# Another layout of keys for seven of sixteen head pairs, a fourth tile for the attention weights, and weight loads issued by ScalarE

## The chip, the cores and the metric

The kernel runs on one core of a Trainium2 chip. The metric is the time of one execution in microseconds (us), as the device measures it; of several executions the median counts. A profile of one execution, taken by the hardware profiler, stands beside the times; its span runs from the first to the last recorded instruction. In it PE is TensorE's matmuls, PEld its weight loads, DVE VectorE, ACT ScalarE, POOL GpSimd, and SP SyncE, whose queue issues DMAs here. A "q" behind an engine's name (SPq) means its sequencer, which issues DMAs and waits on semaphores.

## The reference

Three stages follow each other. Cut to what matters:

```python
# q, k, v: batch 4, heads 8, sequence 576, head dimension 64
q_rot, k_rot = rotate(q), rotate(k)                      # rotary positions
scores = q_rot @ k_rot.T / 8
attn = softmax(scores)
x = (attn @ v), heads side by side                       # 2304 tokens x 512
h = x @ w_in; g = max(0.01 * h, h); x2 = g @ w_out       # 512 -> 2048 -> 512
# each token goes to the one of 8 experts with the largest logit
out[token] = gate[token] * (relu(x2 @ w1[e]) @ w2[e])    # 512 -> 1024 -> 512
```

`w_in` and `w_out` come as 64-bit floats. All matmuls are made of high and low parts, so that the result is as good as in 32-bit floats.

## The kernel before

One program in three parts. Up to about 660 us of the span it runs attention, with the first dense network ("MoE units" in the code's names, `m_...`) woven in from about 180 us on; then the rest of the dense network; from about 795 us on the experts. The change is in the first part.

Attention takes the heads in 16 pairs, `g` = 0 to 15, and each pair in nine units of 128 query rows, `u` = 0 to 8, so there are 144 units. A program written out by a planner in Python takes one step for each unit (`step`, where a string of letters sets the order inside a step). In step i it issues: the score matmuls of unit i+1 (`a_scores`), the row maximum of unit i on DVE (`a_max`), the exponentials of unit i-1 on ACT (`a_exp`), the high part of its weights on ACT (`a_hi`, into a tile `P`) and the low part on DVE (`a_lo`, into the same tile), a DMA transpose of that tile into a tile `PT` (`a_transpose`, on SP's queue), and the product with the values of unit i-4 (`a_pv`). `P` has three buffers. So the high part of one unit can't be written before the transpose of the unit three before it has read its tile.

Beside the steps, jobs run in small pieces that the planner places where its budgets for ACT, DVE and POOL (rates per step) allow:

- `prep(g)` stages a pair: it loads q, k and v (`raw`, 640 KB and 320 KB), rotates and scales q and k on POOL, DVE and ACT, and writes high and low parts, all 16-bit, into a tile `stg` of 20 blocks of 128 x 128. Two DMA transposes of ten blocks each turn it: one to `kt` (keys) and one to `stk` (queries). Each head's scores need the keys' 64 rows twice, above each other, since the stacked high and low queries fill 128 rows. So four DMAs copy from `kt` into `stk`, 160 KB each. After them `load(g + 1, 2)` issues the next pair's load.
- `weights(i)`, four of them side by side, each with one buffer `raw{i}`: they take turns at 32 slices of 512 KB, 16 of `w_in` and 16 of `w_out`. Each is loaded by a DMA on SP's queue, decoded from 64-bit floats on ACT and DVE (`decode`), scaled, and split into a high and a low part on ACT and DVE (`w_in`) or ACT and POOL (`w_out`).

Each engine works its instructions off in the order of the program. On SP's queue stand, in the planner's order, the loads of weight slices, the loads of q, k and v, the transposes of all kinds and the copies.

Of the kernel before, what the change touches and what calls it, by code (L numbers as in the profile page):

```python
# [52 lines left out]
NMERGED = 60  # L53
ADDG = 0
HI_A1 = 1
TICK2 = 3
RATE1 = dict(A=2, V=1.8, G=1.4)
RATE2 = dict(A=2, V=2.1, G=1.6)
# [43 lines left out]
def attention_moe_kernel(ctx: ExitStack, tc: tile.TileContext, qkv, w_in, w_out, emb, tau, w1, w2,  # L102
# [83 lines left out]
    def decode(raw):  # L186

        hw, lw = raw[:, :, 1], raw[:, :, 0]
        yield Piece(A=1.2, tick=M.tick + (TICK2 if M.unit else TICK))
        nc.scalar.activation(out=hw.bitcast(F32), in_=hw.bitcast(F32), func=AF.Copy, scale=2.0 ** -112)  # L190

        nc.scalar.activation(out=lw, in_=lw, func=AF.Identity, scale=2.0 ** -29 * (1 - 2.0 ** -20), bias=half)
        yield Piece(V=0.6)
        nc.vector.scalar_tensor_tensor(out=lw, in0=hw, scalar=3, in1=lw, op0=ALU.logical_shift_left, op1=ALU.bitwise_or)
        yield Piece(V=0.6)
        nc.vector.scalar_tensor_tensor(out=lw, in0=hw, scalar=0x80000000, in1=lw, op0=ALU.bitwise_and, op1=ALU.bitwise_or)
        return lw.bitcast(F32)
# [3 lines left out]
    def weights(i):  # L201
        while slices:
            f, o = slices.popleft()
            raw = wp.tile([128, 512, 2], U32, name=f"raw{i}")
            if o:
                nc.sync.dma_start(out=raw.rearrange("p f t -> p (f t)"), in_=w_out32[128 * f:128 * f + 128, :])
                r = yield from decode(raw)
                yield Piece(A=0.52)
                nc.scalar.activation(out=wo[:, 0, f], in_=r, func=AF.Copy)
                yield Piece(G=1.2)  # L210
                nc.gpsimd.tensor_tensor(out=wo[:, 1, f], in0=r, in1=wo[:, 0, f].bitcast(F32), op=ALU.subtract)
            else:
                nc.sync.dma_start(out=raw.rearrange("p (c f) t -> p c (f t)", c=4),
                                  in_=w_in32[:, 256 * f:256 * f + 256].rearrange("(c p) f -> p c f", p=128))
                w = yield from decode(raw)
                sq = small.tile([128, 1], F32, name="wsq", bufs=NW)
                yield Piece(A=0.61)
                nc.scalar.activation(out=junk[:, 0:512], in_=w, func=AF.Square, accum_out=sq)
                pb = yield from total(sq, 1)
                yield Piece(must=True, V=0.2)  # L220
                s = _pow2(nc, small, pb[:, 0:1], 1, uw[:, f:f + 1])
                nc.vector.tensor_scalar(out=uw01[:, f:f + 1], in0=uw[:, f:f + 1], scalar1=0.01, scalar2=None, op0=ALU.mult)
                hi = wi[:, 0, :, 128 * f:128 * f + 128]
                wv = w.rearrange("p (c f) -> p c f", c=4)
                if WHI:
                    yield Piece(V=0.34)
                    nc.vector.tensor_scalar(out=hi, in0=wv, scalar1=s, scalar2=None, op0=ALU.mult)
                else:
                    yield Piece(A=0.61)
                    nc.scalar.activation(out=hi, in_=wv, func=AF.Copy, scale=s)  # L230
                yield Piece(V=0.6)
                nc.vector.scalar_tensor_tensor(out=wi[:, 1, :, 128 * f:128 * f + 128], in0=wv, scalar=s, in1=hi, op0=ALU.mult, op1=ALU.subtract)
            M.wdone[o].add(f)
            yield Piece()

    def m_ready():
        if M.unit == len(munits):
# [134 lines left out]
    def prep(g):  # L372
# [34 lines left out]
            return s3  # L407


        def stacks():  # L410
            stg = qkp.tile([128, 4, 5, 128], F16, name="stg")
            s2 = stg.rearrange("p s c x -> p (s c x)")
            qhi = s2[:, 0:1408].rearrange("p (h x) -> p h x", h=2)[:, :, 0:640].rearrange("p h (c x) -> p h c x", c=5)[:, :, :, 0:64]
            return (s2, qhi, stg[:, 2].rearrange("p c (h x) -> p h c x", h=2), [stg[:, 0, :, 64:128], stg[:, 1, :, 0:64]],
                    [stg[:, 3, :, 64 * h:64 * h + 64] for h in range(2)])

        def hi(out, t):
            if g and (HIQ, HIK)[t]:
# [8 lines left out]
        if g == 0:  # L427
            rope_s(1)
            rope_s(0, nc.vector)
            for t in range(3):  # L430
                square(t)
            rope_c(0)
            add(0)
            pb = ps_h()
            nc.tensor.matmul(pb[:, 0:3], lhsT=ones, rhs=sq, start=True, stop=True)
            s3 = scales(pb)
            s2, qhi, khi, qlo, klo = stacks()
            hi(qhi, 0)
            rope_c(1)
            add(1)  # L440
            hi(khi, 1)
            lo(klo, 1, khi)
            lo(qlo, 0, qhi)
        else:
            yield Piece(A=0.72, G=1.64, at=max(i0 - EARLY, 0), tick=M.loaded + TLOAD)
            square(0)
            rope_s(0)
            yield Piece(A=0.72, V=0.74, G=1.64)
            square(1)
            rope_c(0)  # L450
            rope_s(1)
            yield Piece(A=0.72, V=0.74)
            square(2)
            add(0, nc.gpsimd if g < ADDG else nc.vector)
            yield Piece(V=0.74)
# [6 lines left out]
            s2, qhi, khi, qlo, klo = stacks()  # L462
            yield Piece(A=1.44)
            hi(qhi, 0)
            hi(khi, 1)
            yield Piece(V=0.93)
            lo(klo, 1, khi)
            yield Piece(V=0.93)
            lo(qlo, 0, qhi)
        yield Piece(at=i0 - 2)  # L470
        kt = stp.tile([128, 2, 640], F16, name="kt", bufs=1)
        nc.sync.dma_start_transpose(out=kt.rearrange("p s (c x) -> p (s c) x", c=5), in_=s2[:, 1280:2560])
        yield Piece(at=i0 - 1)

        stk = stp.tile([128, 6, 640], F16, name="stk")
        nc.sync.dma_start_transpose(out=stk[:, 0:2].rearrange("p s (c x) -> p (s c) x", c=5), in_=s2[:, 0:1280])
        for h in range(2):
            for z in range(2):
                nc.sync.dma_start(out=stk[64 * z:64 * z + 64, 2 + 2 * h:4 + 2 * h], in_=kt[64 * h:64 * h + 64])
        pairs[g] = (stk, s3, sc, v16)  # L480
        if g + 1 < 4 * B:
            load(g + 1, 2)
# [16 lines left out]
    def a_scores(g, u):  # L499
# [3 lines left out]
        for n in range(2):  # L503
            ks = slice(288 * n, 288 * n + 288)
            for h, c0, m, o in todo:
                for a in range(2):
                    nc.tensor.matmul(ps[o:o + m, n, 0:288], lhsT=stk[:, h, c0:c0 + m], rhs=stk[:, 2 + 2 * h + a, ks], start=(a == 0), stop=(a == 1))  # L507
        return ps

    def a_max(g, u, ps):  # L510
# [790 lines left out]
```

## Time and profile before

| | |
|---|---|
| median of 3 executions | 1064.49 us (1061.05 to 1064.89) |
| the profiled execution: its time, its span | 1062.26 us, 1060.5 us |
| busy over the span: PE, DVE, ACT, POOL | 83%, 73%, 71%, 34% |
| SP's DMA queue: time of its packets on 16 engines | 54.9% of the span |

The shares are means over three unlike parts. They say nothing of which engine ends a stage last; that is read from stretches of the span, given below as "A to B us", counted from its start.

### The profile page before, as it was taken

How to read it: one execution, taken by the hardware profiler on the slowest of the kernel's cores; microseconds unless marked ns; L12 is line 12 of the kernel's file. 1: busy time of each engine (PE TensorE's matmuls, PEld its weight loads, DVE VectorE, ACT ScalarE, POOL GpSimd, SP SyncE). 2: the span in 40 equal slices, each digit the busy share in tenths (PEclk: the TensorE clock that was granted, in tenths of full speed). 3: DMA queues.
4: the chain of work that ended last, by engine and by line, in shares of the span. 5: the costliest groups of instructions: out<-in, count | busy, mean ns of one | idle time of the engine just before them, and what ended most of it. 6: DMA issues, size and time to landing. Idle time of an engine off the chain costs nothing. (4 is left out here: it accounts for less than half of the span.)

```text
span 1060.5 us, 19876 instructions
## 1 busy us (share of the span) xinstructions
PE 882.0 (83%) x6737; PEld 709.4 (67%) x6737; DVE 773.9 (73%) x1564; ACT 755.8 (71%) x1439; POOL 360.6 (34%) x414
## 2 busy tenths in 40 slices
PE   1455454777888899989898899999999899999997
PEld 1344243565666787767677677778877778888885
DVE  6988798778867874767768766313476999999893
ACT  6987687777767774877777677535345888888883
POOL 1333323252443452544444533322233361211111
PEclk9995555989989999999999999999999999999999
DMA  7899889788487694696795784301152111115190
GB/s 227 192 219 243 194 165 214 171 178 196 91 163 159 120 180 98 122 177 125 140 198 126 125 162 91 66 1 41 31 180 101 40 61 40 51 50 199 34 334 33
DMA packets 269005, 141.41 MB, mean 133 GB/s; under 512 B 236248, under 2 KB 244696, under 8 KB 268897
## 3 DMA queue, kind: packets, MB, share of 16 engines
q1 hardware_dynamic: 265696, 130.11, 54.9%
q0 software_dynamic: 3200, 9.97, 2.9%
q8 instruction: 55, 0.90, 0.4%
q14 instruction: 54, 0.43, 0.1%
HBM read 120.04 MB, written 10.49 MB: 123 GB/s over the span
## 5 line engine op out<-in xcount | busy, mean ns | idle before, releaser
L266 PE MATMUL h<-xT,wi 128*128 128x256 f16 (+1 forms) x1920 | 218.2, 265 | 36.9 <-DVE g L278 31.2
L266 PEld LDWEIGHTS <-wi 128*128 128x128 f16 x1920 | 170.6, 100 | 83.5 <-issue 63.8
L286 POOL TENSOR_TENSOR gl<-g,gh 128x256 fp32r<-128x256 f32 x144 | 110.7, 769 | 317.2 <-ACT gh L282 293.5
L297 PE MATMUL acc<-wo,gh 128*128 128x512 f32 x576 | 196.6, 423 | 0.0
L531 DVE SCALAR_TENSOR_TENSOR P<-E,P 128x576 f16<-128x576 f32 x144 | 127.6, 886 | 92.7 <-ACT P L525 91.8
L552 PE MATMUL o<-v,PT 128*128 128x65 f16 (+3 forms) x1770 | 104.1, 216 | 66.3 <-DMA PT<-P 46.0
L552 PEld LDWEIGHTS <-PT 128*128 128x128 f16 (+1 forms) x1770 | 92.5, 112 | 85.2 <-DMA PT<-P 58.9
L507 PE MATMUL S<-stk 128*128 128x288 f16 (+1 forms) x640 | 115.4, 332 | 36.4 <-ACT E L519 34.5
L278 DVE SCALAR_TENSOR_TENSOR g<-h,uw,g 128x256 f32<-128x256 f32 (+1 forms) x160 | 71.2, 453 | 100.0 <-ACT g L274 99.5
L282 ACT ACTIVATE gh<-g 128x256 fp32r<-128x256 f32 x144 | 59.9, 416 | 94.7 <-DVE g L278 94.1
L525 ACT ACTIVATE P<-E 128x576 f16<-128x576 f32 x144 | 98.2, 682 | 40.1 <-DMA PT<-P 36.5
L519 ACT ACTIVATE E<-S,amx,sc 128x576 f32<-128x576 f32 x144 | 117.9, 818 | 4.9 <-DVE E L514 4.8
L274 ACT ACTIVATE g<-h,uw 128x256 f32<-128x256 f32 (+1 forms) x160 | 69.4, 444 | 72.6 <-PE h L266 68.1
L514 DVE TENSOR_SCALAR_CACHE_REDUCE E<-S,sc 128x576 f32<-128x576 f32 x144 | 116.5, 809 | 0.7 <-PE S L507 0.2
L297 PE MATMUL acc<-wo,gl 128*128 128x512 f32 x288 | 115.6, 401 | 0.0
L297 PEld LDWEIGHTS acc<-wo,gh 128*128 128x128 f32 x576 | 100.9, 193 | 18.6 <-issue 2.5
L507 PEld LDWEIGHTS <-stk 128*128 128x128 f16 (+1 forms) x640 | 58.1, 112 | 54.2 <-issue 39.2
L940 POOL DMA_INDIRECT out<-eo,idi x18 | 25.3, 1405 | 152.8 <-ACT eo L938 142.0
L390 POOL TENSOR_TENSOR t<-raw,tab 128x320 f32<-128x320 f32 x62 | 63.5, 1054 | 13.2 <-DMA raw<-in_qkv 10.1
L297 PEld LDWEIGHTS acc<-wo,gl 128*128 128x128 f32 x288 | 55.2, 192 | 13.7 <-POOL gl L286 0.9
L587 POOL TENSOR_TENSOR x<-xo,rd 128x128 f32<-128x128 f32 (+1 forms) x33 | 20.9, 632 | 102.7 <-DVE rd L579 80.3
L929 PE MATMUL h<-w,hth 128*128 128x512 f32 x176 | 55.4, 396 | 0.4 <-ACT hth L913 0.4
(232 smaller groups left out, 1754.8 us busy)
## 6 DMA issues: line engine op xcount, KB each, us to landing
rb<-in_w SPq DMA_DIRECT2D x78, 512.0 KB
ra<-in_w SPq DMA_DIRECT2D x76, 512.0 KB
stk<-kt SPq DMA_DIRECT2D x64, 160.0 KB
raw<-in_qkv SPq DMA_DIRECT2D x15, 640.0 KB
raw<-in_w_in SPq DMA_DIRECT2D x16, 512.0 KB
raw<-in_w_out SPq DMA_DIRECT2D x16, 512.0 KB
raw<-in_qkv SPq DMA_DIRECT2D x18, 320.0 KB
x2s<-x SPq DMA_DIRECT2D x18, 256.0 KB
```

Of the source, the lines that this page charges most:

```text
L266: nc.tensor.matmul(m.h[:, c0:c1], lhsT=wi[:, a, c, 128 * f:128 * f + 128], rhs=xT[j][:, 4 * b_ + c, 0:c1 - c0], start=(n == 0), stop=(n == ...
L274: nc.scalar.activation(out=m.g[:, c0:c1], in_=m.h[:, c0:c1], func=AF.Copy, scale=uw[:, f:f + 1])
L278: nc.vector.scalar_tensor_tensor(out=m.g[:, c0:c1], in0=m.h[:, c0:c1], scalar=uw01[:, f:f + 1], in1=m.g[:, c0:c1], op0=ALU.mult, op1=ALU.max)
L286: nc.gpsimd.tensor_tensor(out=m.gl, in0=m.g, in1=m.gh.bitcast(F32), op=ALU.subtract)
L297: nc.tensor.matmul(M.acc[t], lhsT=g_[:, tt], rhs=wo[:, a, f], start=(f == 0 and n == 0), stop=(f == NF - 1 and n == 2))
L390: eng.tensor_tensor(out=t2[t][:, :, :, o:o + 32], in0=raw[:, t, :, :, i:i + 32], in1=sn[:, :, o:o + 32].unsqueeze(1).to_broadcast([128, 2, ...
L507: nc.tensor.matmul(ps[o:o + m, n, 0:288], lhsT=stk[:, h, c0:c0 + m], rhs=stk[:, 2 + 2 * h + a, ks], start=(a == 0), stop=(a == 1))
L514: nc.vector.tensor_scalar(out=e.rearrange("p (a b) -> p a b", a=2), in0=ps[:, :, 0:288], scalar1=pairs[g][2][:, 1:2], scalar2=None, op0=AL ...
L519: nc.scalar.activation(out=e.rearrange("p (a b) -> p a b", a=2), in_=ps[:, :, 0:288], func=AF.Exp, scale=sc[:, 0:1], bias=mx)
L525: nc.scalar.activation(out=p[:, 0:576], in_=e, func=AF.Copy, scale=P_UP)
L531: nc.vector.scalar_tensor_tensor(out=p[:, 576:1152], in0=e, scalar=P_UP, in1=p[:, 0:576], op0=ALU.mult, op1=ALU.subtract)
L552: nc.tensor.matmul(o[ob:ob + m, oc + z:oc + z + w], lhsT=pt[:, i, q0:q0 + m], rhs=v16[:, i, h, c:c + w], start=(n == 0), stop=(n == len(to ...
```

## The change

Three edits and what they bring with them:

- Pairs 0 to 6 (`g < WIDE`) take a narrow layout. `stg` gets five groups of five blocks. The high keys of a head stand twice side by side there, the second time by a copy on DVE (`k2`); the low keys of both heads share one group. One DMA transpose of 25 blocks makes the whole of `stk`; `kt` and the four copies are gone for these pairs. The second score matmul of each couple then contracts over 64 rows (the high queries with the low keys) and no longer over 128; the number of matmuls is the same. The product of low queries and low keys, which the wide layout includes, is left out there. Pairs 7 to 15 are as before.
- The 32 loads of weight slices are issued on ACT's queue. The piece that issues one stands a tick later than before, and the piece behind it a tick less.
- `P` has four buffers.

```diff
+WIDE = 7
...
-        yield Piece(A=1.2, tick=M.tick + (TICK2 if M.unit else TICK))
+        yield Piece(A=1.2, tick=M.tick + (TICK2 if M.unit else TICK) - 1)
...
-                nc.sync.dma_start(out=raw.rearrange("p f t -> p (f t)"), in_=w_out32[128 * f:128 * f + 128, :])
+                nc.scalar.dma_start(out=raw.rearrange("p f t -> p (f t)"), in_=w_out32[128 * f:128 * f + 128, :])
...
-                nc.sync.dma_start(out=raw.rearrange("p (c f) t -> p c (f t)", c=4),
+                nc.scalar.dma_start(out=raw.rearrange("p (c f) t -> p c (f t)", c=4),
                                   in_=w_in32[:, 256 * f:256 * f + 256].rearrange("(c p) f -> p c f", p=128))
...
             M.wdone[o].add(f)
-            yield Piece()
+
+            yield Piece(tick=M.tick + 1)
...
+        wide = g >= WIDE
+
         def stacks():
-            stg = qkp.tile([128, 4, 5, 128], F16, name="stg")
+            stg = qkp.tile([128, 5, 5, 128], F16, name="stg")
...
+            khi = stg[:, 2].rearrange("p c (h x) -> p h c x", h=2) if wide else stg[:, 2:4, :, 0:64]
+            return (s2, qhi, khi, [stg[:, 0, :, 64:128], stg[:, 1, :, 0:64]],
+                    [stg[:, 3 if wide else 4, :, 64 * h:64 * h + 64] for h in range(2)], stg[:, 2:4, :, 64:128])
...
+            else:
+                yield Piece(V=1.2)
+                lo(qlo, 0, qhi)
+                nc.vector.tensor_copy(out=k2, in_=khi)
+                yield Piece(V=0.93)
+                lo(klo, 1, khi)
+        if wide:
+            yield Piece(at=i0 - 2)
+            kt = stp.tile([128, 2, 640], F16, name="kt", bufs=1)
+            nc.sync.dma_start_transpose(out=kt.rearrange("p s (c x) -> p (s c) x", c=5), in_=s2[:, 1280:2560])
         yield Piece(at=i0 - 1)
         stk = stp.tile([128, 6, 640], F16, name="stk")
-        nc.sync.dma_start_transpose(out=stk[:, 0:2].rearrange("p s (c x) -> p (s c) x", c=5), in_=s2[:, 0:1280])
-        for h in range(2):
-            for z in range(2):
-                nc.sync.dma_start(out=stk[64 * z:64 * z + 64, 2 + 2 * h:4 + 2 * h], in_=kt[64 * h:64 * h + 64])
+        if wide:
...
+        else:
+            nc.sync.dma_start_transpose(out=stk[:, 0:5].rearrange("p s (c x) -> p (s c) x", c=5), in_=s2)
...
+                else:
+                    hr = slice(64 * h, 64 * h + 64)
+                    nc.tensor.matmul(ps[o:o + m, n, 0:288], lhsT=stk[:, h, c0:c0 + m], rhs=stk[:, 2 + h, ks], start=True, stop=False)
+                    nc.tensor.matmul(ps[o:o + m, n, 0:288], lhsT=stk[hr, h, c0:c0 + m], rhs=stk[hr, 4, ks], start=False, stop=True)
...
-        p = pep.tile([128, 2 * S], F16, name="P", bufs=3)
+        p = pep.tile([128, 2 * S], F16, name="P", bufs=4)
```

The change also moves instructions. On SP's queue, where pair 3 is staged (during pair 2), there stood before:

```order
L535 DMA_TRANSPOSE PT<-P 128x9x128 x6
L472 DMA_TRANSPOSE kt<-stg 128x10x128
L213 DMA raw_1245<-in_w_in 128x4x256
L476 DMA_TRANSPOSE stk<-stg 128x10x128
L479 DMA stk<-kt 64x1280 x4
L370 DMA raw_1265<-in_qkv 128x1280
L206 DMA raw_1267<-in_w_out 128x1024
L535 DMA_TRANSPOSE PT<-P 128x9x128
L213 DMA raw_1312<-in_w_in 128x4x256
```

In the changed kernel there stands, at the same place:

```order
L558 DMA_TRANSPOSE PT<-P 128x9x128 x7
L497 DMA_TRANSPOSE stk<-stg 128x25x128
L372 DMA raw_1147<-in_qkv 128x1280
L558 DMA_TRANSPOSE PT<-P 128x9x128 x2
L512 DMA v_117<-v_117 64x1040
```

Eight issues stood between two transposes of `PT`; now two do. The group stands behind the transpose of unit 20, no longer of unit 21, so pairs are staged one or two steps earlier. The dense network's units stand at the same steps as before throughout.

On ACT's queue, at the start of the program, there stood before (`en` and `em` belong to the experts' directions, `raw_120` and `raw_124` hold q, k and v of pair 0):

```order
L629 ACT_TABLE_LOAD
L629 ACTIVATE warm<-ones 128x1
L630 ACTIVATE junk,en_140<-em 8x512
L631 ACTIVATE en_140<-en_140 8x1
L632 ACT_TABLE_LOAD
L632 ACTIVATE warm<-ones 128x1
L385 ACTIVATE junk,sq_148<-raw_120 128x640 x2
```

In the changed kernel the first four loads of slices come ahead of the same instructions:

```order
L214 DMA raw_132<-in_w_in 128x4x256
L207 DMA raw_134<-in_w_out 128x1024
L214 DMA raw_136<-in_w_in 128x4x256
L207 DMA raw_138<-in_w_out 128x1024
L652 ACT_TABLE_LOAD
L652 ACTIVATE warm<-ones 128x1
```

On SP's queue these four stood behind the loads of pair 0; now they stand in another queue and behind nothing.

Where the first unit's exponentials stand on ACT, its queue in the changed kernel reads (`raw_183` holds q and k of pair 1):

```order
L231 ACTIVATE wi<-raw_132,ps 128x4x128
L214 DMA raw_236<-in_w_in 128x4x256
L210 ACTIVATE wo<-raw_138 128x512
L387 ACTIVATE junk,sq_201<-raw_183 128x640
L207 DMA raw_260<-in_w_out 128x1024
L231 ACTIVATE wi<-raw_136,ps 128x4x128
L214 DMA raw_263<-in_w_in 128x4x256
L387 ACTIVATE junk,sq_201<-raw_183 128x640
L542 ACTIVATE E<-S,amx,sc 128x576
```

Three loads of slices, into buffers that DVE and POOL have to give free first, now stand ahead of the first exponentials (L542); before, none stood on this queue.

## Rows read from the trace of the kernel before

**Rows 1.** Three stretches: length, busy us of PE, PEld, DVE, ACT, POOL; clock, DMA share, GB/s.

```profile
24.00:200.00 176.00, 89.90 (x843) 64.80 (x843) 152.17 (x348) 135.35 (x269) 56.91 (x58) 0.69 0.87 200
200.00:305.00 105.00, 81.37 (x786) 64.81 (x784) 79.29 (x181) 77.34 (x166) 38.95 (x44) 0.95 0.82 168
305.00:660.00 355.00, 322.00 (x2809) 261.11 (x2809) 252.03 (x593) 257.40 (x560) 155.70 (x208) 0.98 0.72 139
```

**Rows 2.** Waits of DVE, 24 to 200 us: total, times, longest.

```profile
DVE P L531 <- ACT P L525: 16.3, 8, 5.4
```

**Rows 3.** Waits of ACT, 24 to 200 us.

```profile
ACT P L525 <- DMA PT<-P: 17.9, 8, 5.8
```

**Rows 4.** Waits of PE, 24 to 200 us.

```profile
PE o L552 <- DMA PT<-P: 35.6, 13, 8.3
```

**Rows 5.** SP's queue in time, where pair 3 is staged: start, us.

```profile
114.92 1.40 SPq L472 DMA_TRANSPOSE kt<-stg  x1
...
118.68 2.94 SPq L479 DMA_DIRECT2D stk<-kt  x4
121.66 0.65 SPq L370 DMA_DIRECT2D raw<-in_qkv  x1
122.36 1.46 SPq L206 DMA_DIRECT2D raw<-in_w_out  x1
123.92 1.91 SPq L535 DMA_TRANSPOSE PT<-P  x1
```

**Rows 6.** All engines in time, 129.9 to 131.2 us: start, busy.

```profile
130.24 0.94 PE L552 MATMUL o<-v,PT 128*128 128x65 f16 x14 [8.32 <-DMA PT<-P]
...
130.28 0.68 ACT L525 ACTIVATE P<-E 128x576 f16<-128x576 f32 x1 [5.81 <-DMA PT<-P]
...
130.99 0.83 DVE L531 SCALAR_TENSOR_TENSOR P<-E,P 128x576 f16<-128x576 f32 x1 [5.43 <-ACT P L525]
```

**Rows 7.** Waits of ACT, 200 to 305 us.

```profile
ACT P L525 <- DMA PT<-P: 5.2, 1, 5.2
```

**Rows 8.** Waits of ACT, 305 to 660 us.

```profile
ACT P L525 <- DMA PT<-P: 13.4, 4, 4.2
```

**Rows 9.** DMA packets from 105.5 to 112 us: packets, MB, share.

```profile
q1 hardware_dynamic: 2368, 0.59, 47.8%
```

**Rows 10.** DMA packets from 18 to 21.3 us.

```profile
DMA packets 783, 0.67 MB, mean 204 GB/s; under 512 B 569, under 2 KB 569, under 8 KB 783
...
q1 hardware_dynamic: 783, 0.67, 86.1%
```

**Rows 11.** DMA packets from 144 to 150 us.

```profile
DMA packets 1548, 0.67 MB, mean 111 GB/s; under 512 B 1184, under 2 KB 1548, under 8 KB 1548
...
q1 hardware_dynamic: 1548, 0.67, 50.3%
```

**Rows 12.** SP's queue in time, from the start on.

```profile
14.12 1.48 SPq L472 DMA_TRANSPOSE kt<-stg  x1
...
17.78 2.45 SPq L479 DMA_DIRECT2D stk<-kt  x4
```

**Rows 13.** PE in time, first score matmuls.

```profile
21.29 1.11 PE L507 MATMUL S<-stk 128*128 128x288 f16 x4 [1.23 <-DMA stk<-kt]
```

**Rows 14.** Issues of one line, first w_in's: ns least, median, most.

```profile
L213 SPq DMA_DIRECT2D raw<-in_w_in x16: 385/532/1306, 4.0 to 242.5; - x16
```

**Rows 15.** The same of w_out's loads.

```profile
L206 SPq DMA_DIRECT2D raw<-in_w_out x16: 328/501/1923, 4.5 to 243.1; - x16
```

**Rows 16.** Groups by line and shape: DVE's copies.

```profile
L1118 DVE COPY x2U<-h 128x512 f32<-128x512 f32 x1 | 0.7, 692 | 0.7 <-PE h L1114 0.7
...
L768 DVE COPY ca<-c 128x8 f32<-128x8 f32 x1 | 0.4, 354 | 0.0
```

**Rows 17.** Groups by line and shape: score matmuls over 128 rows.

```profile
L507 PE MATMUL S<-stk 128*128 128x288 f16 x512 | 102.2, 332 | 32.8 <-ACT E L519 30.9 <-DMA stk<-kt 1.6
```

**Rows 18.** ACT in time, from the start on.

```profile
6.98 0.74 ACT L385 ACTIVATE junk<-raw 128x640 bf16<-128x640 f32 x1 [1.42 <-DMA raw<-in_qkv]
```

More of the change, by code (lines that the diff above doesn't have):

```diff
@@ L407, in scales @@
             return s3
+        wide = g >= WIDE
         def stacks():
-            stg = qkp.tile([128, 4, 5, 128], F16, name="stg")
+            stg = qkp.tile([128, 5, 5, 128], F16, name="stg")
             s2 = stg.rearrange("p s c x -> p (s c x)")
             qhi = s2[:, 0:1408].rearrange("p (h x) -> p h x", h=2)[:, :, 0:640].rearrange("p h (c x) -> p h c x", c=5)[:, :, :, 0:64]
-            return (s2, qhi, stg[:, 2].rearrange("p c (h x) -> p h c x", h=2), [stg[:, 0, :, 64:128], stg[:, 1, :, 0:64]],
-                    [stg[:, 3, :, 64 * h:64 * h + 64] for h in range(2)])
+            khi = stg[:, 2].rearrange("p c (h x) -> p h c x", h=2) if wide else stg[:, 2:4, :, 0:64]
+            return (s2, qhi, khi, [stg[:, 0, :, 64:128], stg[:, 1, :, 0:64]],
+                    [stg[:, 3 if wide else 4, :, 64 * h:64 * h + 64] for h in range(2)], stg[:, 2:4, :, 64:128])
         def hi(out, t):
@@ L436, in prep @@
             s3 = scales(pb)
-            s2, qhi, khi, qlo, klo = stacks()
+            s2, qhi, khi, qlo, klo, k2 = stacks()
             hi(qhi, 0)
@@ L441, in prep @@
             hi(khi, 1)
+            lo(qlo, 0, qhi)
+            nc.vector.tensor_copy(out=k2, in_=khi)
             lo(klo, 1, khi)
-            lo(qlo, 0, qhi)
         else:
@@ L461, in prep @@
             s3 = scales(pb)
-            s2, qhi, khi, qlo, klo = stacks()
+            s2, qhi, khi, qlo, klo, k2 = stacks()
             yield Piece(A=1.44)
@@ L465, in prep @@
             hi(khi, 1)
[L466 to L472, printed above, removed]
+            if wide:
+                yield Piece(V=0.93)
+                lo(klo, 1, khi)
+                yield Piece(V=0.93)
+                lo(qlo, 0, qhi)
+            else:
+                yield Piece(V=1.2)
+                lo(qlo, 0, qhi)
+                nc.vector.tensor_copy(out=k2, in_=khi)
+                yield Piece(V=0.93)
+                lo(klo, 1, khi)
+        if wide:
+            yield Piece(at=i0 - 2)
+            kt = stp.tile([128, 2, 640], F16, name="kt", bufs=1)
+            nc.sync.dma_start_transpose(out=kt.rearrange("p s (c x) -> p (s c) x", c=5), in_=s2[:, 1280:2560])
         yield Piece(at=i0 - 1)
         stk = stp.tile([128, 6, 640], F16, name="stk")
-        nc.sync.dma_start_transpose(out=stk[:, 0:2].rearrange("p s (c x) -> p (s c) x", c=5), in_=s2[:, 0:1280])
-        for h in range(2):
-            for z in range(2):
-                nc.sync.dma_start(out=stk[64 * z:64 * z + 64, 2 + 2 * h:4 + 2 * h], in_=kt[64 * h:64 * h + 64])
+        if wide:
+            nc.sync.dma_start_transpose(out=stk[:, 0:2].rearrange("p s (c x) -> p (s c) x", c=5), in_=s2[:, 0:1280])
+            for h in range(2):
+                for z in range(2):
+                    nc.sync.dma_start(out=stk[64 * z:64 * z + 64, 2 + 2 * h:4 + 2 * h], in_=kt[64 * h:64 * h + 64])
+        else:
+            nc.sync.dma_start_transpose(out=stk[:, 0:5].rearrange("p s (c x) -> p (s c) x", c=5), in_=s2)
         pairs[g] = (stk, s3, sc, v16)
@@ L505, in a_scores @@
             for h, c0, m, o in todo:
-                for a in range(2):
-                    nc.tensor.matmul(ps[o:o + m, n, 0:288], lhsT=stk[:, h, c0:c0 + m], rhs=stk[:, 2 + 2 * h + a, ks], start=(a == 0), stop=(a == 1))
+                if g >= WIDE:
+                    for a in range(2):
+                        nc.tensor.matmul(ps[o:o + m, n, 0:288], lhsT=stk[:, h, c0:c0 + m], rhs=stk[:, 2 + 2 * h + a, ks], start=(a == 0), stop=(a == 1))
+                else:
+                    hr = slice(64 * h, 64 * h + 64)
+                    nc.tensor.matmul(ps[o:o + m, n, 0:288], lhsT=stk[:, h, c0:c0 + m], rhs=stk[:, 2 + h, ks], start=True, stop=False)
+                    nc.tensor.matmul(ps[o:o + m, n, 0:288], lhsT=stk[hr, h, c0:c0 + m], rhs=stk[hr, 4, ks], start=False, stop=True)
         return ps
```

## Prediction

> **What bounds the kernel now.** I read the busy times by stage first, since the page's shares mix three parts. From 24 to 200 us (the first five pairs, with most of the slices) DVE works 152.17 of 176 us and is the engine nearest to its limit; ACT works 135.35, PE only 89.90, and the DMA engines are busy 87% of the time [rows 1]. From 200 us on PE leads, 81.37 of 105 us and then 322.00 of 355, so what DVE or ACT loses there costs only where PE runs dry. The change touches the first stage most, and there the question is what makes DVE wait in its remaining 23.8 us.
>
> The waits of each engine answer that. DVE waits 16.3 us for the high part of P on ACT, eight times [rows 2]; ACT waits 17.9 us before the same instruction, eight times, for a DMA transpose of P to have read its buffer [rows 3]; PE waits 35.6 us for the transposed tile [rows 4]. The longest case shows that this is one event: at 130.24 us PE, at 130.28 ACT and then DVE go on, after 8.32, 5.81 and 5.43 us [rows 6]. So late transposes cost the first stage up to 16.3 us.
>
> Why that one is late stands on SP's queue. Its issue is at 123.92 us; ahead of it, from 114.92 on, go the transposes of keys and queries, four copies, the next pair's load and weight slices [rows 5]. From 114.92 to 130.24 are 15.3 us. I price the work between from stretches where little else runs. Two transposes of P alone take 47.8% of 6.5 us [rows 9], so 1.55 us of all DMA engines each for nine blocks, 0.173 per block. From 18 to 21.3 us 2.84 us are busy; 569 small packets at the same price per packet (1.55 us for 1184) are 0.74, and the 214 others, from the copies, 2.1 [rows 10], which makes 2.5 us for all 256 packets of a pair's four copies. From 144 to 150 us 3.02 us are busy, 1.55 of it in 1184 small packets, so 364 packets of a w_in slice take 1.47 and its 512 packets 2.07 us [rows 11]. A pair's load of 640 KB is at that rate 2.6. The burst is then 20 blocks 3.5, copies 2.5, load 2.6, two slices 4.1, P 1.55: 14.3 of the 15.3 us. It is the queue's work itself that makes the transpose late.
>
> **The change, part by part.** *The burst.* After it: 25 blocks 4.3, load 2.6, P 1.55. A transpose has a fixed part too: `kt` is issued at 14.12 us and the copies that read it go out at 17.78 [rows 12], 3.7 us, of which ten blocks are 1.7; so 1.9 fixed. Together 10.4 us if the slices in their own queue stay out of the way, 14.5 if both share the engines with it in full. Against 15.3 that saves 4.9 or 0.8; I take the middle, 2.8. Four pairs are staged in this stage: 11 us. The fourth P buffer lets ACT and DVE run one unit further before a late transpose stops them; but PE needs the same transpose for the product and has the next scores behind it in its order, so DVE would soon wait for PE instead. I give it 2. Together 13 of the 16.3 us; ends 3 (four times 0.8) and 16.
>
> The Trainium skill says ("DMA: Bandwidth & Descriptors", "Issuing engines are not separate DMA queues") that DMAs of all issuing engines run on the same 16 DMA engines, so that another issuer saves only the sequencer's time; by it alone the burst would be the 14.5 us case. The same page ("Queues, rings and completion order") says that a DMA engine takes turns between the queues that have work, by which small transposes would not stand behind a whole slice; that would be nearer to 10.4. No row here shows two such queues at once.
>
> *The fourth P buffer later.* ACT waits for transposes 5.2 us once from 200 to 305 us and 13.4 us in four waits up to 660 [rows 7, 8]. PE leads there and has its own work queued, so I count 3 of these 18.6; ends 0 and 12.
>
> *Loads on ACT.* An issue of a slice took SP a median of 532 ns (w_in) or 501 (w_out), from 328 up to 1923 when the queue was full [rows 14, 15]. ACT has no such row. Nothing better is known than the same 0.52 us: 28 loads behind the start make 14.5 us. What can hide them is ACT's idle time, without its waits for P 22.7 us in the first stage and 22.5 in the second (176 - 135.35 - 17.9 and 105 - 77.34 - 5.2) [rows 1, 3, 7]. Those are waits in the middle of a cycle with DVE, so an issue before an exponential delays the next DVE step. I take a third, 4.8 us; ends 0 and 14.5. That SP loses these issues is in the burst already.
>
> *The copy of high keys.* One per narrow pair, 128 x 640, 16-bit to 16-bit. DVE's other copies took 692 ns for 512 elements a row and 354 for eight [rows 16]. I take 0.45 us; six behind the start are 2.7, and as DVE is the nearest to its limit I count 2.5; ends 1 and 4.
>
> *Matmuls over 64 rows.* No score matmul over 64 rows stands in the trace; over 128 rows it takes 332 ns [rows 17]. I take the same. Of 40 per pair, 20 change. At half the time they would give PE 3.3 us a pair, and as much would be lost if each cost 0.16 us more; PE is idle half of the first stage, which hides either. For pairs 4 to 6, which meet the dense network, it could be 5 us to either side. The planner's two earlier steps for staging move no unit of the dense network, so I count them as nothing.
>
> *The start.* The first four slices no longer wait behind pair 0's loads, they run beside them, 8.3 us of DMA at 2.07 each; and their four issues, 2.1 us, come ahead of the table loads on ACT. ACT's second square waits for k until 6.98 us [rows 18] and all of pair 0 hangs on it. Against that, `kt`, copies and their waits from 14.12 to the first scores at 21.29 us [rows 12, 13], 7.2 us, become a copy and one transpose, 0.45 + 1.9 + 4.3 = 6.65, but begin only when the last low part is written, about 1 us later. And the third slice load on ACT has DVE to wait for, with the first exponentials behind it. I take a loss of 2 us; ends a gain of 1 and a loss of 5.
>
> **The sum** from the profiled execution's 1062.26 us: -13 - 3 + 4.8 + 2.5 + 2 = -6.7, so 1055.6. That execution ran 2.2 us below the median of 1064.49; on the median it is 1057.8, 0.6% less.
>
> **Rivals.** *The engines stay shared.* If the slices cost a burst as much as before, only 0.8 us is saved each time: -3 - 1.5 + 4.8 + 2.5 + 2 = +4.8, 1069 on the median, no difference that tells. The first of the two rules of the Trainium skill above leads here. For it: the DMA engines are 87% busy in this stage [rows 1]. Against it: between bursts they stand idle (two transposes in 6.5 us [rows 9]), and slices can go there.
>
> *ScalarE is held by its loads* (slower). A load that ACT issues must wait until DVE or POOL has given the buffer free, and exponentials, high parts and evacuations of the values' product wait behind it. With all 14.5 us of issues on the path and 0.5 us of such waiting for half of them, 7 us: -13 - 3 + 21.5 + 2.5 + 2 = +10, 1074.5. The change loses once a load costs the path over 0.41 us on average (16 us of gain less 4.5 of other costs, over 28 loads), where I count 0.17. For it: ACT has 135 of 176 us busy, and SP's issues went up to 1.9 us. Against it: the planner puts the issue a tick behind the last reader.
>
> *All the lateness goes and the issues hide.* -16 - 10 + 2.5 + 1 + 0 is -22, 1042: the second stage too is then freed of the waits for P. For it: 14.3 of a burst's 15.3 us were queue work. Against it: DVE is at 152 of 160 us without its waits, and I know no stage that ran fuller.
>
> **How the numbers follow.** A measurement of this kernel tells about 0.5% from no change, here 1059.2 and 1069.8. My forecast (1052 to 1064) gets 0.42, the large gain 0.20, shared engines 0.20, ScalarE held 0.18. Faster: two thirds of the forecast and the large gain, 0.48. Slower: ScalarE held and a third of the shared case, 0.24. Same: the rest, 0.28. The range takes most of the large gain and of the held case: 1043 to 1075; the forecast's own is 1052 to 1064.
>
> **What would show it.** Right: ACT's waits for P fall from 17.9 us to under 6 before 200 us, PE's for the transposed tile from 35.6 to under 15; the transpose behind a pair's staging is free within 11 us of the 25-block one's issue; unit 36's maximum comes some 7 us earlier. Wrong: ACT shows waits at the lines of the loads, or its idle time before exponentials grows by 0.5 us a load (held); PE still waits over 25 us for transposed tiles (shared); the first scores come later than 24 us (start).

## The result and the profile after

The changed kernel takes 1076.07 us (median of 4 runs, 1074.97 to 1077.73), the kernel before 1064.41 on the same chip (4 runs). The ratio is 1.0118, with a 95% interval of 1.0093 to 1.0142: **slower by 1.2%**, where 0.6% faster was predicted. The profiled execution took 1075.84 us, its span is 1074.0, against 1060.5 before.

The busy times by stage, columns as in [rows 1]:

```profile
24.00:200.00 176.00, 105.50 (x748) 56.95 (x749) 149.81 (x339) 134.03 (x260) 59.32 (x54) 1.00 0.81 186
200.00:305.00 105.00, 89.16 (x780) 63.59 (x776) 80.01 (x184) 75.63 (x164) 41.34 (x45) 0.97 0.77 145
305.00:660.00 355.00, 323.06 (x2804) 261.11 (x2804) 244.62 (x587) 254.41 (x551) 152.79 (x205) 0.97 0.75 142
```

The first stage got less done: 748 matmuls and 339 instructions of DVE in the same 176 us, where there were 843 and 348, and the DMA engines are less busy, 81% and not 87%. The clock column must be read with care here. Its first record in this trace is at 199.9 us; the fourteen short products of a unit took 0.94 us before that (at 98.73 us, below), as long as in [rows 6], where the trace before shows a granted 0.5. So PE ran at the lower level, 1.2 GHz, there too.

Of the waits from 24 to 200 us these answer to [rows 2 to 4], DVE's and then PE's:

```profile
DVE E L537 <- PE S L530: 11.0, 4, 3.9
DVE raw L397 <- POOL t L392: 8.0, 3, 4.5
...
DVE P L554 <- ACT P L548: 0.2, 1, 0.2
```

```profile
PE S L529 <- ACT E L542: 26.4, 19, 3.2
PE o L575 <- DMA PT<-P: 23.5, 7, 7.0
```

Before, DVE's waits for POOL and for PE's scores were these:

```profile
DVE raw L395 <- POOL t L390: 3.0, 1, 3.0
...
DVE E L514 <- PE S L507: 0.2, 1, 0.2
```

ACT's wait of 17.9 us for a free P is gone altogether, and with it all but 0.2 of DVE's 16.3. But PE still waits 23.5 us for transposed tiles, seven times up to 7.0. Behind the held product stand the next scores, and DVE waits 11.0 us for those, where it waited 0.2. Most of the stall has only changed its name. DVE's wait for POOL, which rotates the next pair's q and k, rose as well, from 3.0 to 8.0 us.

Where the time goes, by the start of a unit's row maximum on DVE in the profiled executions. The third column has the narrow layout and four tiles of P without the loads on ACT (experiment e8); the others come below. The profiled execution of e8 was the slowest of its four and that of e9 the fastest of its ten, so these two columns end 2.4 us apart where the medians are 13.1 apart:

| us | before | e8 | e9 | e13 | after |
|---|---|---|---|---|---|
| unit 0 | 23.9 | 23.4 | 25.8 | 24.5 | 28.6 |
| unit 9 | 58.6 | 59.7 | 62.1 | 62.3 | 66.3 |
| unit 18 | 91.7 | 94.4 | 96.8 | 103.3 | 107.3 |
| unit 27 | 132.9 | 127.7 | 131.4 | 141.7 | 147.7 |
| unit 36 | 173.3 | 165.0 | 173.2 | 179.0 | 187.7 |
| end of span | 1060.5 | 1053.8 | 1056.2 | 1060.6 | 1074.0 |

By unit 18 the changed kernel is 15.6 us behind before, and it ends 13.5 behind: the whole loss arises in the first pairs. Against e8 it loses 5.1 at the start, some 6 between units 9 and 18 and some 7 between 18 and 27.

What happens there is seen where pair 2 of the heads is prepared, during pair 1 (staged at unit 12, that is with twelve transposes of P ahead). First SP's queue, then ACT's:

```profile
83.92 1.24 SPq L558 DMA_TRANSPOSE PT<-P  x1
85.21 7.16 SPq L497 DMA_TRANSPOSE stk<-stg  x1
92.41 0.58 SPq L372 DMA_DIRECT2D raw<-in_qkv  x1
93.11 1.34 SPq L558 DMA_TRANSPOSE PT<-P  x1
```

```profile
84.72 0.68 ACT L548 ACTIVATE P<-E 128x576 f16<-128x576 f32 x1
84.73 0.39 ACTq L214 DMA_DIRECT2D raw<-in_w_in  x1
...
85.15 0.69 ACTq L207 DMA_DIRECT2D raw<-in_w_out  x1
```

ACT issues two slices 0.48 and 0.06 us before SP issues the 25-block transpose. The packets of 88 to 89 us, by queue (q10 is ACT's, q1 SP's): their number, their MB, and their time as a share of the 16 engines' time, which goes past 100% because packets overlap:

```profile
q10 hardware_dynamic: 271, 0.35, 118.4%
q1 hardware_dynamic: 2, 0.00, 0.1%
```

Up to 87.4 us SP's queue moves the transpose of P that was issued at 83.92. For the 2.7 us after that it moves next to nothing, while the slices run; whether the next transpose's packets were ready by then, the trace does not show. They start at 90.1 us, 4.9 after the issue, which takes SP 7.16 us. In e8 they start 1.3 to 1.4 us after the issue for pairs 1 to 4, and the issue takes 3.8 to 4.0. The transpose of P behind it goes out at 93.11, and PE gets it after 6.07 us of waiting:

```profile
98.73 0.94 PE L575 MATMUL o<-v,PT 128*128 128x65 f16 x14 [6.07 <-DMA PT<-P]
```

### The profile page after: what moved, and what is told of

It is laid out like the page before. It is cut to its first block, busy times and chain, and to the rows that moved or that the text cites. A ratio compares the mean times of both kernels' runs of the same rounds, so it can differ in the third digit from the quotient of the medians.

```text
span 1074.0 us, 19816 instructions
## 1 busy us (share of the span) xinstructions
PE 917.3 (85%) x6737; PEld 709.7 (66%) x6737; DVE 771.6 (72%) x1571; ACT 759.5 (71%) x1439; POOL 365.6 (34%) x414
## 5 line engine op out<-in xcount | busy, mean ns | idle before, releaser
L288 POOL TENSOR_TENSOR gl<-g,gh 128x256 fp32r<-128x256 f32 x144 | 113.3, 786 | 329.5 <-ACT gh L284 294.7
L554 DVE SCALAR_TENSOR_TENSOR P<-E,P 128x576 f16<-128x576 f32 x144 | 125.1, 869 | 67.0 <-ACT P L548 66.7
L542 ACT ACTIVATE E<-S,amx,sc 128x576 f32<-128x576 f32 x144 | 118.0, 820 | 2.8 <-DVE E L537 2.2
L529 PE MATMUL S<-stk 128*128 128x288 f16 (+1 forms) x140 | 52.2, 373 | 28.3 <-ACT E L542 28.3
L526 PE MATMUL S<-stk 128*128 128x288 f16 (+1 forms) x360 | 53.9, 290 | 6.5 <-ACT E L542 6.3
L610 POOL TENSOR_TENSOR x<-xo,rd 128x128 f32<-128x128 f32 (+1 forms) x33 | 23.7, 718 | 96.0 <-DVE rd L602 80.2
```

What stands on the lines that cost most here:

```text
L288: nc.gpsimd.tensor_tensor(out=m.gl, in0=m.g, in1=m.gh.bitcast(F32), op=ALU.subtract)
L542: nc.scalar.activation(out=e.rearrange("p (a b) -> p a b", a=2), in_=ps[:, :, 0:288], func=AF.Exp, scale=sc[:, 0:1], bias=mx)
L554: nc.vector.scalar_tensor_tensor(out=p[:, 576:1152], in0=e, scalar=P_UP, in1=p[:, 0:576], op0=ALU.mult, op1=ALU.subtract)
```

## Experiments

Ratios are to the kernel before on the same chip, with 95% intervals. "Ticks" are the two tick numbers of the change, in `decode` and behind `wdone`.

### One part at a time: e1 to e4

e1 has only the fourth tile of P:

```diff
-        p = pep.tile([128, 2 * S], F16, name="P", bufs=3)
+        p = pep.tile([128, 2 * S], F16, name="P", bufs=4)
```

> The kernel before with four buffers of P, nothing else. Both theories expect little: ACT's waits before the high part of P (17.9 us before 200 us, 18.6 after) go to nearly nothing, but PE still waits for the same transposes and DVE then waits for PE's scores instead: 1058 to 1064 us, ratio 0.994 to 1.000.

Measured: 1053.75 us, 0.9911 (0.9890 to 0.9932), faster than expected. PE still waits 39.1 us for transposed tiles from 24 to 200 us, more than the 35.6 of [rows 4], but ACT not at all:

```profile
PE o L552 <- DMA PT<-P: 39.1, 16, 8.5
```

By the starts of the maxima 4.5 us are gained up to unit 36, the rest later.

e2 has only the loads on ACT's queue, with the ticks:

```diff
-        yield Piece(A=1.2, tick=M.tick + (TICK2 if M.unit else TICK))
+        yield Piece(A=1.2, tick=M.tick + (TICK2 if M.unit else TICK) - 1)
...
-                nc.sync.dma_start(out=raw.rearrange("p f t -> p (f t)"), in_=w_out32[128 * f:128 * f + 128, :])
+                nc.scalar.dma_start(out=raw.rearrange("p f t -> p (f t)"), in_=w_out32[128 * f:128 * f + 128, :])
...
-            yield Piece()
+            yield Piece(tick=M.tick + 1)
```

> The kernel before with the loads of slices on ACT's queue (and the two ticks that go with it), wide keys, three buffers of P. Theory A (the loss comes from the 25-block transpose, which holds SP's queue for 4 to 8 us and makes the next pair's load late): without it the queue of SP is only relieved, 1056 to 1066 us. Theory B (the loss comes from the loads: they stand in ACT's order and run beside the bursts and beside pair 0's loads): most of the loss is here already, 1071 to 1077 us.

Measured: 1080.04 us, 1.016 (1.0131 to 1.0188). This part alone, the loads with their ticks, makes the loss.

e3 has only the narrow layout (`WIDE = 7` and all that hangs on it):

> The changed kernel with the loads of slices back on SP's queue (with the ticks of before) and three buffers of P, so narrow keys alone. Theory A: the loss is here, 1068 to 1077 us, and the 25-block transpose takes SP 4 us or more. Theory B: a little faster than before, since a burst has 1.7 us less work of the DMA engines, 1058 to 1064 us.

Measured: 1054.9 us, 0.9929 (0.9900 to 0.9959). So the 25-block transpose by itself, which one theory blamed, is not the loss; up to 200 us its issue takes SP 3.8 to 4.8 us here.

e4 is the change without the narrow layout (the edits of e1 and e2):

> The changed kernel without narrow keys: loads of slices on ACT and four buffers of P. Theory A: about as fast as before or faster, 1053 to 1065 us. Theory B: 1068 to 1076 us, near the changed kernel.

Measured: 1080.85 us, 1.0177 (1.0145 to 1.0208), no different from e2. No gain of the fourth tile shows beside the loads on ACT.

### The loads taken apart: e5 to e7

e5 has the ticks alone, the loads stay on SP's queue (the first and the third hunk of e2):

> The kernel before with the two changed ticks of the slices alone; loads stay on SP's queue. Theory A has fallen: narrow keys alone are faster. Theory B in two readings. B1 (place in the planner's order): the ticks pull the slices' work into steps where DVE and the bursts are full, so the loss is here without any load on ACT: 1072 to 1080 us. B2 (own queue): behind ACT's order the slices run ahead of a pair's copies and load instead of behind them; with SP's queue as before the loss is gone: 1058 to 1066 us.

Measured: 1068.18 us, 1.0058 (1.0041 to 1.0075), a small loss between the two readings.

e6 is e2, but the first four slices stay on SP's queue:

```diff
+                (nc.sync if f < 2 else nc.scalar).dma_start(out=raw.rearrange("p f t -> p (f t)"), in_=w_out32[128 * f:128 * f + 128, :])
```

> Loads of slices on ACT's queue, but the first four on SP's as before, wide keys, three buffers of P. If the start (slices beside pair 0's loads, first scores 4.7 us later) is the cause, 1064 to 1068 us. If the place of the later slices ahead of the bursts is (B2), still 1074 to 1080 us, with first scores at about 24 us again.

Measured: 1077.6 us, 1.014 (1.0096 to 1.0184); the interval overlaps that of e2. The start is not what costs most.

e7 is the kernel before with 32 more DMAs of 512 bytes that ACT issues, one ahead of each slice:

```diff
+            dummy = small.tile([128, 1], F32, name="dm", bufs=4)
+            nc.scalar.dma_start(out=dummy, in_=ident[:, 0:1])
```

> The kernel before with 32 loads of one column (512 bytes) to a scratch tile issued by ACT at the places where a slice is loaded; the slices stay on SP. It adds the issues to ACT without their transfers. If ScalarE's issue time is the price (0.34 to 0.39 us each, 11 us in all), 1070 to 1075 us. If it hides beside running ACTIVATEs (B2), 1062 to 1066 us.

Measured: 1061.51 us, 0.9985 (0.9971 to 0.9999). An issue by itself costs ACT nothing that can be measured, though each shows 338 ns (median) in its queue. A slice's wait for its buffer is not in this.

### Without the loads on ACT: e8

e8 is the change with SP's loads and the ticks of before (the edits of e1 and e3):

> Narrow keys and four buffers of P, slices on SP's queue: the change without its loads on ACT. Alone they gave 8 and 9 us. If the two take away different waits, 1045 to 1050 us; if they take away the same ones (both shorten waits for late transposes), 1051 to 1055 us.

Measured: 1050.10 us, 0.9876 (0.9849 to 0.9903), faster than both kernels. In its profile ACT waits for no transpose of P from 24 to 200 us, and PE waits 14.6 us for transposed tiles:

```profile
PE o L575 <- DMA PT<-P: 14.6, 8, 5.3
```

### Queue against ticks: e9, e10, e13

e9 is e8 with the loads on ACT's queue, ticks as before (only `nc.sync` to `nc.scalar` in the two loads):

> The changed kernel with the slice loads on ACT's queue, but the two pieces around an issue at the ticks of before: slices are issued 0 to 3 units later than in the changed kernel, for instance beside units 15, 16, 16, 18 and 22, 23 where the changed kernel has 13, 13, 15, 16 and 20, 21; the pairs are staged at units 12, 20, 29 in both. Theory 'place' (slices cost time because they are issued in the step of a staging and so run ahead of it and of the transposes of P): most of the loss goes, 1052 to 1060 us. Theory 'queue' (any slice that ACT issues runs ahead of what SP has queued, wherever it stands): 1066 to 1074 us, the changed kernel less the 5 us that the ticks cost by themselves.

Measured: 1063.24 us, 1.0003 (0.9983 to 1.0023), between the two expectations. The profiled execution took 1058.07, the fastest of ten. Its stall is another one than that of 88 us above:

```profile
136.82 0.94 PE L575 MATMUL o<-v,PT 128*128 128x65 f16 x14 [6.98 <-DMA PT<-P]
```

ACT issues two slices at 123.17 and 123.83 us. The packets from 127 to 134 us, by queue:

```profile
q10 hardware_dynamic: 583, 0.84, 66.9%
q1 hardware_dynamic: 919, 0.23, 62.7%
```

Here both queues run at once, with about equal time of packets. SP's 919 packets are less than one transpose of P (1152); in e8 3688 packets, nearly all of transposes, went through in these microseconds. By the packets three transposes in a row landed 9.3, 10.8 and 8.7 us after their issue; in e8 none of this stage took over 8.

ScalarE is held by its loads here too. Two of its waits from 24 to 200 us:

```profile
ACT xo L585 <- DVE wi L233: 4.4, 2, 2.2
...
ACT junk L219 <- POOL wo L212: 2.5, 1, 2.5
```

Evacuations of the values' product (`xo`) and a square (`junk`) need nothing of `wi` or `wo`. They stand right behind a load whose buffer DVE or GpSimd has still to read. With one exponential of 0.9 us that makes 7.8 us.

e10 is the kernel before with the loads on ACT's queue and the ticks of before:

> The kernel before with the loads on ACT's queue and nothing else, the ticks as before. Theory 'place': 1062 to 1068 us, since only the issuing engine changes and the steps stay. Theory 'queue': 1073 to 1077 us, the 1080 of loads with ticks less the 5 to 6 of the ticks alone on SP's queue.

Measured: 1084.93 us, 1.0217 (1.0186 to 1.0248), worse than with the ticks. Two waits of ACT from 24 to 200 us stand out:

```profile
ACT P L525 <- DMA PT<-P: 32.4, 5, 11.1
ACT E L519 <- POOL wo L211: 5.4, 3, 2.6
```

The first is the late transposes again, 32.4 us where it was 17.9 [rows 3]. The second is new: exponentials wait for GpSimd's low part of a slice, which they don't use. They stand behind a load that needs that slice's buffer. So ScalarE is held by its loads here. In e2, with the new ticks, no exponential waits so.

e13 is the change with the loads back on SP's queue, the new ticks kept:

> The changed kernel with the slice loads back on SP's queue, everything else as changed, the ticks too (slices beside units 12, 12, 14, 15 and 19, 20, 21, 22; pairs staged at 12, 20, 29). With queue and ticks independent of each other it is 1076 - 13 = 1063 us, 13 above the version with the old ticks. If the ticks hurt only because a slice in a queue apart gets ahead of the staging, they cost here little: 1050 to 1056 us. If the step in which a slice stands is all that counts and not its queue: 1070 to 1076 us.

Measured: 1063.52 us, 1.002 (1.0003 to 1.0037), the first expectation. With narrow pairs and four tiles the two halves of the edit add up within the noise (they did not all run on one chip; as ratios to before the halves are 1.4% and 1.3%, together 2.4%):

| us | ticks of before | new ticks |
|---|---|---|
| loads on SP | 1050.10 (e8) | 1063.52 (e13) |
| loads on ACT | 1063.24 (e9) | 1076.07 (after) |

In the wide kernel with three tiles they do not: there the new ticks lose some 5 us with the loads on SP (e5) and gain some 5 with the loads on ACT (e10 to e2).

The ticks' share is seen on SP's queue where pair 2 is staged, first in e8 and then in e13:

```profile
73.60 3.76 SPq L497 DMA_TRANSPOSE stk<-stg  x1
77.40 0.59 SPq L372 DMA_DIRECT2D raw<-in_qkv  x1
78.16 1.39 SPq L558 DMA_TRANSPOSE PT<-P  x1
```

```profile
81.25 4.41 SPq L497 DMA_TRANSPOSE stk<-stg  x1
85.72 0.57 SPq L372 DMA_DIRECT2D raw<-in_qkv  x1
86.32 0.43 SPq L214 DMA_DIRECT2D raw<-in_w_in  x1
86.87 0.44 SPq L207 DMA_DIRECT2D raw<-in_w_out  x1
87.83 2.02 SPq L558 DMA_TRANSPOSE PT<-P  x1
```

With the new ticks two slices stand in the very step of the staging (unit 12); with the ticks of before they come two and three units later. In the order of the programs (counted by transposes of P on SP's queue, by exponentials on ACT's, which are one ahead) the slices nearest to the stagings at units 12, 20 and 29 stand beside 14, 15, 15, then 22, 22, then 29, 29 in e8; beside 12, 12, then 19, 20, 21, then 29, 29 in e13; beside 13, 13, then 20, 21, then 30, 30 in the changed kernel. From the issue of `stk` to the landing of the transpose of P behind it, by the packets, are 9.1 us in e8 (to 82.7) and 12.7 in e13 (to 94.0), and 12.8 in the changed kernel (85.21 to 98.0). PE's wait in that place, e8 and then e13:

```profile
83.46 0.94 PE L575 MATMUL o<-v,PT 128*128 128x65 f16 x14 [1.38 <-DMA PT<-P]
```

```profile
94.66 0.94 PE L575 MATMUL o<-v,PT 128*128 128x65 f16 x14 [6.01 <-DMA PT<-P]
```

So slices ahead of this transpose cost it 3.6 or 3.7 us, and PE 4.6 or 4.7, in either queue. (In the changed kernel a third slice, issued at 91.20, runs in that stretch too.) The same time at the stagings of pairs 1 to 4, found by counting SP's packets of 256 bytes in the order of the issues, 128 to a block; for the kernel before it starts with the issue of `kt`:

| us | pair 1 | pair 2 | pair 3 | pair 4 | mean |
|---|---|---|---|---|---|
| before | 11.9 | 11.6 | 14.7 | 12.4 | 12.7 |
| e8 | 10.2 | 9.1 | 9.0 | 12.2 | 10.1 |
| e9 | 9.4 | 9.7 | 9.8 | 10.9 | 10.0 |
| e13 | 9.5 | 12.7 | 10.7 | 13.1 | 11.5 |
| after | 11.1 | 12.8 | 13.2 | 13.1 | 12.6 |

With the ticks of before, the queue apart makes no staging longer (e8, e9); its cost there lies elsewhere. From e13 to the changed kernel, by the starts of the maxima, the queue costs 4.0 us at unit 0 and still 4.1 at unit 22, then 6.0 at unit 27, 8.7 at unit 36 and 14.8 at unit 72. So about a third of it is the start, and none of it arises where pair 2 is staged.

### Slices held back, and another queue: e11 and e14

e11 is the change, but no slice is issued from the last step of a staging to one behind it:

```diff
-            yield Piece(tick=M.tick + 1)
+            yield Piece(tick=M.tick + 1, when=lambda: M.tick > M.hold)
...
+                M.hold = 10 ** 6
                 yield Piece(V=0.93)
...
+        M.hold = M.tick + 1
         vjobs.append(Job(prep_v(g, v16, rawv, s3)))
```

> The changed kernel, but no slice is issued from the last step of a pair's staging to one step behind it (slices beside units 22, 22, 22, 23 and 31, 31, 31, 31 where the changed kernel has 20, 21, 22, 23 and 27, 27, 30, 30). Theory 'place': the stalls of 6 to 8 us at the first four stagings shrink to those of the narrow kernel with loads on SP, 1053 to 1062 us. Theory 'queue': bunches of two to four slices now stand ahead of the transposes of P instead, 1070 to 1078 us.

Measured: 1083.86 us, 1.0189 (1.0161 to 1.0218), above both expectations and against my theory of the place alone. Held back, the slices come in bunches of two to four, two units behind the staging, and then run ahead of the transposes of P. PE's waits from 24 to 200 us:

```profile
PE o L578 <- DMA PT<-P: 31.6, 5, 10.1
```

e14 is e8 with the slices issued by GpSimd (`nc.gpsimd.dma_start`):

> Narrow pairs, four tiles of P and the ticks of before, with the slices issued by GpSimd. On ACT's queue this took 1063.2 us, on SP's 1050.1. Theory 'queue' (slices in any queue apart get ahead of the transposes): 1059 to 1067 us. Theory 'ScalarE held' (exponentials behind a load that waits for its buffer): 1048 to 1055 us, as ScalarE issues nothing. Above 1067 us GpSimd's own work, the rotation of the next pair, would be held by its loads.

Measured: 1073.17 us, 1.0113 (1.0047 to 1.0179). That is the third case of the expectation. ScalarE issues nothing here, and yet it is slower than e9. But an issue takes GpSimd 0.5 to 0.8 us of its own time, and 12 of the 20 us by which its profile ends behind that of e8 come after unit 33, so this does not settle how the 13 us of ACT's queue divide.

### The narrow layout where PE leads: e12, e15, e16

These are e8 with another number of narrow pairs (`WIDE = 16`, `4`, `5`). In e12 the product of low queries and low keys is left out for all pairs.

> Narrow layout for all sixteen pairs, four tiles of P, loads on SP's queue; the product of low queries with low keys is left out for all pairs. The version with seven narrow pairs took 1050.1 us. If the narrow layout gains by fewer DMAs in the burst, pairs 7 to 15 lie where PE leads and little is to be had: 1047 to 1051 us. If the 25-block transpose's issue of up to 8 us on SP holds transposes of P where PE leads: 1052 to 1060 us.

Measured: 1061.21 us, 0.998 (0.9968 to 0.9991), 11 us above e8. The stage from 305 to 660 us, e8 and then e12:

```profile
305.00:660.00 355.00, 321.51 (x2799) 260.97 (x2799) 242.97 (x587) 254.28 (x553) 149.08 (x204) 0.97 0.74 138
```

```profile
305.00:660.00 355.00, 349.29 (x2748) 254.87 (x2746) 243.09 (x583) 250.24 (x543) 147.11 (x200) 1.00 0.66 125
```

PE is busy 27.8 us more with fewer matmuls. Most of it is seen in the score matmuls of one unit, e8's wide pair and then e12's narrow one:

```profile
440.34 0.65 PE L526 MATMUL S<-stk 128*128 128x288 f16 x4
```

```profile
443.60 0.29 PE L529 MATMUL S<-stk 128*128 128x288 f16 x1
443.82 0.29 PE L530 MATMUL S<-stk 64*128 64x288 f16 x1
444.05 0.30 PE L529 MATMUL S<-stk 128*128 128x288 f16 x1
444.27 0.29 PE L530 MATMUL S<-stk 64*128 64x288 f16 x1
444.50 0.73 PE L299 MATMUL acc<-wo,gh 128*128 128x512 f32 x2
```

Four over 128 rows take 0.65 us together. Four that alternate between 128 and 64 rows take 0.29 each in both cases, but start 0.22 to 0.23 us apart, 0.96 together: 0.31 us more per unit. Some 80 units lie in this stretch, which makes 25 of the 27.8 us. How much of the 11 us that is, and how much the 25-block transposes of these pairs, is not divided.

> Narrow layout for pairs 0 to 3 only, four tiles of P, loads on SP's queue with the ticks of before; with seven narrow pairs 1050.1 us. A unit's score matmuls take PE 0.97 us instead of 0.65, so 0.32 us more, some 3 us for the nine units of a pair. If that counts where PE leads, pairs 5 and 6, and half of 4, give 7 us back, less the longer bursts there: 1043 to 1049 us. If PE's waits hide it there, the lighter bursts are what counts: 1051 to 1056 us.

> The same with pairs 0 to 4 narrow. If the matmuls' starts count: 1045 to 1050 us, for pairs 5 and 6; if the bursts count: 1050 to 1054 us.

Measured: 1050.69 us with four narrow pairs, 0.9888 (0.9845 to 0.9931), and 1047.79 with five, 0.9867 (0.9831 to 0.9903). Neither can be told from seven (0.9876): whether the matmuls' starts already cost in pairs 4 to 6 is left open.

## Why the prediction was wrong

**The step that failed is "Loads on ACT".** It counted 4.8 us for the time of 28 issues, plus 2 us for the start, and put at nothing what the loads do to the work around them. An issue by itself costs nothing that can be measured (e7; in the changed kernel the medians are 386 and 341 ns, overlapping ACT's work as at 84.72 us above). The edit as a whole costs 24.6 us: the other two edits alone are 12.9 us faster than the kernel before (e8), the changed kernel is 11.7 slower. About half of that is the ticks, which I had named in the change and given no term at all; the other half is the queue.

**The ticks.** I saw that pairs are staged one or two steps earlier and counted that at nothing, since no unit of the dense network moves; that slices move by a tick I did not price. Together the two bring slices into the step of a staging: 13.4 us from e8 to e13. In the wide kernel they cost 5.2 us (e5, against 1063.02 of before on that chip).

**The burst in the changed kernel.** I priced it at 10.4 us with the slices out of the way and at 14.5 with the engines shared, and took the middle, 12.45. By the table under e13 it takes 10.1 on average in e8 and 12.6 in the changed kernel, so these prices were near. Wrong was the base of 15.3: it is the longest of four stagings, and measured to PE's start; to the landing that one takes 14.7 and the four 12.7 on average. (Nine issues stood between the two transposes of `PT` there, not eight.) So the changed kernel's bursts are no shorter than before, where I had counted on 2.8 us each, and with 11.1 to 13.2 they miss the 11 that I had named as a sign. The slices take back what the narrow layout saves.

**The queue.** With the ticks of before it costs 13.1 us (e8 to e9). By the Trainium skill ("DMA: Bandwidth & Descriptors", "Issuing engines are not separate DMA queues") all issuers share 16 engines and only the sequencer's time is saved; the trace agrees where pair 2 is staged, with 12.7 and 12.8 us in the two queues. The turns that the same page of the Trainium skill describes ("Queues, rings and completion order") show in e9, 66.9% and 62.7%, but not at 88 us in the changed kernel, 118.4% and 0.1%. How the 13 us divide between the start (2.4 us at unit 0 of e9, 4.0 in the changed kernel), late transposes and ScalarE's standing (7.8 us of its time in e9) is open; e14 does not separate them.

**The burst without the loads, and the fourth tile,** were right in sum. I had -13 - 3 + 2.5 for the copies, -13.5; e8 measured -12.9 (1063.02 to 1050.10). It shows what was announced, no wait of ACT for P (under 6) and 14.6 us of PE for transposed tiles (under 15), where the changed kernel has 23.5. The narrow layout alone gives 8.0 (e3) for -11 + 2.5. The fourth tile alone gives 9.2 us (e1, against 1062.93 of before on that chip), 4.5 up to unit 36 and the rest later, for 2 and 3; beside the narrow layout it adds some 5 (e3 to e8), since the two take away partly the same waits. That the sum came out so near owes something to luck, as the base of the burst was too high. With the new ticks the narrow layout and the fourth tile together give only 4 to 5 (e5 to e13).

**The copy of keys** takes 314 ns, not 450. **The issue of the 25-block transpose** takes SP 3.9 to 7.7 us in the changed kernel, a median of 5.5, which I had not counted; with 3.8 to 4.8 e3 is faster all the same.

**Matmuls over 64 rows** were set at nothing since one takes as long as over 128 rows. That holds (371 and 370 ns), but their starts lie further apart. The price that I gave as the bound of a loss, 0.16 us each, is the one measured (0.31 in e12 for the two of a unit that change). In the first stage, at the lower clock, the four take 1.46 us in e8 and 1.14 before (medians), and PE is busy more with fewer matmuls in the changed kernel; that its waits hide this there is argued, not shown, though e3 is faster all the same.

**The start** lost 4.6 us at the first maximum, within my 5 but over the 2 of the sum; the first scores come at 26.96 us, past the 24 that I had named as a sign. With the loads on SP (e13) only 0.6 of it is left. Two squares on ACT wait for k and v, at 9.26 and 11.69 us, while the four slices run:

```profile
9.26 0.74 ACT L387 ACTIVATE junk<-raw 128x640 bf16<-128x640 f32 x1 [1.57 <-DMA raw<-in_qkv]
...
11.69 0.74 ACT L387 ACTIVATE junk<-raw 128x640 bf16<-128x640 f32 x1 [1.59 <-DMA raw<-in_qkv]
```

**The rivals.** "ScalarE is held" gave 1074.5 and came nearest by number; its mechanism shows in part. In the changed kernel an evacuation of the values' product waits 1.8 us behind a load whose buffer DVE has still to read:

```profile
ACT xo L585 <- DVE wi L233: 1.8, 1, 1.8
```

Two more such waits, ahead of a decoding (1.3) and of a `wi` (0.6), make 3.7 us from 24 to 200 us, where the rival had 7 of waits and 14.5 of issues. In e9 they come to 7.8 us, in e10 exponentials alone wait 5.4. So for the queue's half this rival is not ruled out. "The engines stay shared" had the mechanism of the burst and gave 1069; it lacked what the loads cost outside the bursts and the start.

## What to carry to other kernels

Here a queue apart took bulk loads out from behind small urgent transfers, and thereby let them run ahead of those. Before moving loads, list in the program's order which small transfers the engine that waits will need within the next few microseconds, and price the load into each of them. A number that shifts a planner's pieces by a tick is an edit of its own; run it alone, and look at what it comes to stand beside. Price a stall from all its occurrences, not from the longest. When two shapes of an operation last equally long, compare the distance of their starts as well.

## What the runs showed of the hardware

- Two DMA queues did not take turns everywhere: slices of ACT's queue, issued 0.5 and 0.1 us ahead of a transpose on SP's, had the engines to themselves from 88 to 90 us (q1 0.1% of 88 to 89); whether the transpose was ready is not shown. In e9, where transposes were issued while slices ran, the packets of each queue took about two thirds of the engines' time, overlapping, and three transposes of P took 8.7 to 10.8 us to land.
- Score matmuls that alternate between 128 and 64 rows start 0.22 us apart, those over 128 rows alone 0.12, at 0.29 us each.
- An issue on ACT's queue (medians 0.34 and 0.39 us) runs beside an ACTIVATE; on GpSimd it takes 0.5 to 0.8 us, which the profile counts as that engine's own time.
